# fp32 loads for heads 0 to 3, masks built by query third, and FFN matmuls split into four 32-column tiles, in a block-sparse attention and FFN kernel

## The chip, the cores and the metric

The kernel runs on one core of one Trainium2 chip. The metric is the time that the device measures for one execution, in microseconds (us); lower is better. The profiler's span of an execution is some 2 us shorter than that time. Runs come with a state: "slow" when the time is more than 1.5% above the fastest run of the same kernel, otherwise "fast".

Engines in the profile: PE is TensorE (matmuls), PEld its weight loads, ACT ScalarE, DVE VectorE, POOL GpSimd, SP SyncE, which here issues DMAs only. L214 is a line of the kernel's source; the line numbers differ between kernels.

## The reference

```python
def attention(q, k, v, sampled_blocks):     # q, k, v: (4 batches, 8 heads, 768, 64), fp32
    scores = q @ k^T / 8
    # mask of 32x32 blocks: the diagonal and its neighbours, first and last block row and column,
    # and three blocks per row that sampled_blocks names
    attn = softmax(where(mask, scores, -1e9))
    return attn @ v

def ffn(x, w1, w2, w3, w_out):              # x: (3072 tokens, 512); d_ff = 1024
    return ((x @ w1) * (x @ w2)) @ w3 @ w_out

out = ffn(attention(...) with heads side by side, ...)      # (3072, 512), fp32
```

(Shortened to the formulas.) The mask depends on the sampled blocks, so the kernel has to build it on the chip.

## The kernel before

Everything runs in one program whose order on PE, ScalarE and VectorE is the order of the source. It is a loop of 72 attention steps, 18 for each batch. A step takes four heads, a third of the queries (256) and a third of the keys (256). Loads and the order on GpSimd are left to the scheduler. GpSimd issues the loads of q, k, v and the weights, with a cast from fp32 to bf16.

```python
# step s (cut): scores of this group, then values of the group before, then two pieces of fill
for s, g in enumerate(groups):
    scores(b, t, Q, kp, 0)          # 4 score matmuls for heads 0,1: 64 rows x 128 columns
    scores(b, t, Q, kp, 1)          # 4 for heads 2,3; each call: exp on ScalarE, mask * e on VectorE
    if prev is not None:
        values(*prev)               # 24 matmuls in 128x32 tiles, four heads side by side
        finish(prev)                # after every third group: normalize()
    if b + 1 < B and r in (2, 5, 8, 11):
        load_pair_t(b + 1, (r - 2) // 3)        # next batch: q, k turned by DMA transposes
    if b == 0 and s in (7, 8):
        transposes(0, s - 5)                    # 12 PE transposes and one copy
    pop(0 if s < 3 else 2)                      # fill: weight folding, then the FFN
    prev = g

# normalize(): ln = Ln(d); rec = Exp(-ln)  on ScalarE;  x = o * rec  on VectorE
# The next step's values() overwrite o and d, so they wait for x.

# one FFN piece of the fill (cut): four full 128x128 matmuls of 512 columns
for c in range(4):
    nc.tensor.matmul(p, lhsT=w1_sb[:, c, f * 128:(f + 1) * 128], rhs=x[:, c, :],
                     start=c == 0, stop=c == 3)

# before the first step (cut): block adjacency matrix A (24 x 24) by 21 small VectorE operations,
# expansion G = A * hot (PE, copied by VectorE), then nine masks, each two matmuls and
#     nc.scalar.copy(mask[:, t, kp, :], mp)
```

A "pa" piece of fill is followed by a "pb" piece, and a step takes the two; the "po" pieces are the second product, also two to a step. w3 and w_out are folded into one matrix (wf) first, by fill in the early steps. What is left of the FFN after the last step runs alone: the tail.

The softmax here doesn't subtract the row's maximum and nothing guards it: scores larger than these inputs give would overflow.

## Time and profile before

| | before |
|---|---|
| time, median of 4 runs | 289.2 us (288.57 to 289.72) |
| span of the profiled run | 286.8 us |
| first score matmul | 19.88 us |
| step 5 starts | 33.17 us |
| step 21 starts | 83.91 us |
| step 71, the last, starts | 244.38 us |
| tail, step 71 to the end | 42.4 us |

The checkpoints are read from the trace: a step starts with its first score matmul. FFN pieces begin at step 19 in this kernel, and at step 21 in the changed one.

The windows table of the kernel before (window; its length; busy time of PE, PEld, DVE, ACT and POOL with their instructions; mean clock; DMA share; GB/s) shows the steady part and the tail:

```profile
85.00:240.00 155.00, 153.09 (x1936) 76.76 (x1927) 109.82 (x161) 122.99 (x162) 21.71 (x28) 1.00 0.52 67
240.00:290.00 50.00, 42.57 (x262) 18.79 (x259) 20.05 (x30) 13.74 (x23) 0.00 (x0) 0.96 0.11 43
```

PE is busy 153.09 of 155 us and no other engine is above 123. Busy is not streaming, though. The timeline of PE in one plain step (start, busy time, engine, line, operation, output and inputs, tile rows*columns, operand shapes, count):

```profile
151.28 0.61 PE L214 MATMUL s<-qkt 64*128 64x256 bf16 x8
151.82 0.40 PE L244 MATMUL o<-e,vn 128*32 128x256 bf16 x8
...
152.37 0.28 PE L241 MATMUL d<-e,ones 128*32 128x256 bf16 x4
152.59 1.90 PE L324 MATMUL po<-wf_sb,h 128*128 128x512 bf16 x8
154.42 0.28 PE L214 MATMUL s<-qkt 64*128 64x256 bf16 x2
```

Read the starts. The step is 154.42 - 151.28 = 3.14 us. From single records: four score pairs at 109 ns, six value groups of four tiles at 109 ns (so four 32-column tiles do run side by side), and eight FFN matmuls at 216 ns give 2.82 us. The rest, 0.3 us, is three stops of 0.090 to 0.106 us, one at each change of the tile shape. The Trainium skill, "TensorEngine Tiling (Array Packing)", Key Properties, says that changing the tiling mode drains the engine; it gives no price, and the trace gives one.

Every third step follows a normalise and takes 3.33 us. In the timeline of the kernel before, one such step:

```profile
144.33 0.42 ACT L259 ACTIVATE rec<-ln 128x256 f32<-128x256 f32 x1
144.78 0.69 DVE L260 TENSOR_TENSOR x<-o,rec 128x512 bf16<-128x512 f32 x1
...
144.80 0.61 PE L214 MATMUL s<-qkt 64*128 64x256 bf16 x8
...
145.53 0.40 PE L244 MATMUL o<-e,vn 128*32 128x256 bf16 x8
```

The values start 0.73 us after the scores, where a plain step has 0.54 (151.82 - 151.28): x ends at 145.47, and the values cannot start before. That chain (exp 1.02 us, ln 0.39, rec 0.42, x 0.69) hangs on the *step before*, not on this one's matmuls.

The start, in the timeline of the kernel before (in brackets: idle time before it, and what ended it):

```profile
10.58 0.60 PE L167 MATMUL gp<-hot,Ab 24*24 24x512 bf16 x1 [10.58 <-DVE Ab L161]
...
15.59 4.22 ACT L177 CAST mask<-mp 128x512 bf16<-128x512 f32 x8 [13.57 <-PE mp L175]
...
19.88 1.03 PE L214 MATMUL s<-qkt 64*128 64x256 bf16 x8
```

The adjacency matrix is ready at 10.58 us, the masks hold ScalarE until 19.81, and only then do the scores start.

### The profile page before, as it was taken

Reading aid. Unit: us, or ns where it says so; the run is one execution under the profiler, and the core shown is the slowest. Engines: PE = TensorE matmul, PEld = TensorE weight load, DVE = VectorE, ACT = ScalarE, POOL = GpSimd, SP = SyncE. Lnnn points to the kernel's source line nnn. Section 1 sums busy time; section 2 is a strip of 40 time slices with the busy share of each in tenths; the row PEclk is TensorE's granted clock in tenths of the full one; section 3 lists DMA queues with packets and bytes.
Section 4 is the critical chain, followed back from the end, with each engine's and each line's share of the span. In section 5 each row is a group of like instructions: output and inputs, shape, how many; then the busy total and the mean of one; then the engine's idle time right before and its main releaser. Section 6 shows DMA issues by size and latency. Waiting matters only on the chain.

```text
span 286.8 us, 7359 instructions
## 1 busy us (share of the span) xinstructions
PE 260.8 (91%) x3124; PEld 132.3 (46%) x3124; DVE 183.8 (64%) x296; ACT 188.8 (66%) x250; POOL 71.5 (25%) x105
## 2 busy tenths in 40 slices
PE   0478888898999999999999999999999999999994
PEld 0334555454544454445444554445444544444441
DVE  2616786786767776777677767766776677633332
ACT  1088764776788886888877888768887688611310
POOL 8614489374644820066000000000000000000000
PEclk9986999999999999999999999999999999999998
DMA  7999999999999992399912000121000220003003
GB/s 92 151 190 206 208 174 167 178 119 140 135 167 112 144 109 91 79 118 150 160 73 75 2 2 0 39 75 38 3 2 0 77 75 2 0 37 112 0 29 117
DMA packets 70356, 26.16 MB, mean 91 GB/s; under 512 B 58036, under 2 KB 65204, under 8 KB 70324
## 3 DMA queue, kind: packets, MB, share of 16 engines
q0 software_dynamic: 47632, 14.69, 50.9%
q1 hardware_dynamic: 22692, 11.02, 18.5%
q8 instruction: 24, 0.39, 0.6%
q14 instruction: 8, 0.07, 0.1%
HBM read 29.36 MB, written 6.29 MB: 124 GB/s over the span
## 4 chain that ended last, share of the span: by engine, by line
PE 62%; DMA 12%; ACT 12%; DVE 5%; POOL 5%; issue 3%; POOLq 0%; ACTq 0%
PE pa L303 13%; PE o L244 12%; PE pb L314 12%; DMA w_sb<-in_moe_w_dram 11%; PE po L324 10%; ACT e L219 7%; PE s L214 7%; DVE x L260 4%; PE d L241 4%; PE wp L285 3%; ACT rec L259 3%; ACT ln L257 2%; DMA nt<-in_q_dram 2%; POOL w_sb L99 1%; POOL vn L85 1%
## 5 line engine op out<-in xcount | busy, mean ns | idle before, releaser
L219 ACT ACTIVATE e<-s 128x1024 bf16<-128x1024 f32 x144 | 139.1, 1021 | 47.7 <-PE s L214 47.6
L220 DVE TENSOR_TENSOR e<-e,mask 128x1024 bf16<-128x1024 bf16 x144 | 99.0, 691 | 53.8 <-ACT e L219 53.8
L244 PE MATMUL o<-e,vn 128*32 128x256 bf16 x1152 | 54.7, 277 | 5.4 <-DVE x L260 1.7
L214 PE MATMUL s<-qkt 64*128 64x256 bf16 x576 | 46.8, 277 | 3.5 <-ACT e L219 3.5
L303 PE MATMUL pa<-x,w_sb 128*128 128x512 bf16 x192 | 49.7, 381 | 0.0
L314 PE MATMUL pb<-x,w_sb 128*128 128x512 bf16 x192 | 49.2, 379 | 0.0
L316 DVE TENSOR_TENSOR h<-pb,a 128x512 bf16<-128x512 f32 x48 | 33.1, 690 | 20.9 <-PE pb L314 20.9
L324 PE MATMUL po<-wf_sb,h 128*128 128x512 bf16 x192 | 44.5, 380 | 0.0
L306 ACT CAST a<-pa 128x512 bf16<-128x512 f32 x48 | 28.0, 582 | 22.6 <-PE pa L303 22.2
L241 PE MATMUL d<-e,ones 128*32 128x256 bf16 x576 | 42.5, 275 | 0.0
L214 PEld LDWEIGHTS <-qkt 64*128 64x128 bf16 x576 | 22.8, 95 | 34.7 <-issue 32.0
L244 PEld LDWEIGHTS <-vn 128*32 128x32 bf16 x1152 | 27.5, 96 | 22.0 <-issue 19.2
L314 PEld LDWEIGHTS <-w_sb 128*128 128x128 bf16 x192 | 18.7, 98 | 24.1 <-issue 2.6
L201 POOL DMA_DIRECT2D nt<-in_q_dram x24 | 19.7, 824 | 40.2 <-DMA qkt<-nt 35.9
L324 PEld LDWEIGHTS <-h 128*128 128x128 bf16 x192 | 17.5, 98 | 22.3 <-issue 3.4
L303 PEld LDWEIGHTS <-w_sb 128*128 128x128 bf16 x192 | 15.7, 98 | 21.7 <-issue 8.0
L329 DVE COPY ob<-po 128x512 f32<-128x512 f32 x24 | 16.5, 688 | 10.1 <-PE po L324 10.1
L201 POOL DMA_DIRECT2D nt<-in_k_dram x24 | 19.6, 821 | 4.3 <-DMA qkt<-nt 2.3
L260 DVE TENSOR_TENSOR x<-o,rec 128x512 bf16<-128x512 f32 x24 | 16.6, 692 | 1.6 <-ACT rec L259 0.9
L241 PEld LDWEIGHTS <-ones 128*32 128x32 bf16 x576 | 17.3, 98 | 0.3
L285 PE MATMUL wp<-wo_sb,w3t_sb 128*128 128x512 bf16 x64 | 15.2, 380 | 0.0
L177 ACT CAST mask<-mp 128x512 bf16<-128x512 f32 x9 | 4.8, 587 | 13.7 <-PE mp L175 13.7
(56 smaller groups left out, 106.9 us busy)
## 6 DMA issues: line engine op xcount, KB each, us to landing
out_dram<-ob SPq DMA_DIRECT2D x24, 256.0 KB, 2.0
vn<-in_v_dram POOLq DMA_DIRECT2D x16, 192.0 KB, 5.8
nt<-in_q_dram POOLq DMA_DIRECT2D x24, 96.0 KB, 5.6
nt<-in_k_dram POOLq DMA_DIRECT2D x24, 96.0 KB, 5.6
w_sb<-in_moe_w_dram POOLq DMA_DIRECT2D x8, 256.0 KB, 11.2
w_sb<-in_moe_w_dram POOLq DMA_DIRECT2D x16, 128.0 KB, 5.8
wo_sb<-in_moe_w_out_dram POOLq DMA_DIRECT2D x1, 1024.0 KB, 12.0
qn<-in_q_dram POOLq DMA_DIRECT2D x4, 192.0 KB, 7.2
```

The lines of the kernel that those rows point to most:

```text
L201: nc.gpsimd.dma_start(out=n[:, :, h, :], in_=src[b][:, :, 2 * pr + h, :])
L214: nc.tensor.matmul(s[:, h, k2 * QT:(k2 + 1) * QT], lhsT=qk[64 * h:64 * h + 64, 1, kc * 128:(kc + 1) * 128], rhs=qk[64 * h:64 * h + 64, 0, ...
L219: nc.scalar.activation(e, s, AF.Exp, scale=1.0 / 8.0)
L220: nc.vector.tensor_tensor(e, e, mask[:, t, kp:kp + 1, :].to_broadcast((128, 2, 512)), op=ALU.mult)
L241: nc.tensor.matmul(d[rows, :], lhsT=ones, rhs=rhs, start=first, stop=last, skip_group_check=True)
L244: nc.tensor.matmul(o[rows, part * QT:(part + 1) * QT], lhsT=vn[b, 2 * Q + i][:, h, kc, 32 * part:32 * part + 32], rhs=rhs, start=first and ...
L260: nc.vector.tensor_tensor(X[i][:, 2 * Q:2 * Q + 2, half * QT:(half + 1) * QT], o.rearrange("p (s n) -> p s n", s=2), rec.to_broadcast((128 ...
L303: nc.tensor.matmul(p, lhsT=w1_sb[:, c, f * 128:(f + 1) * 128], rhs=x[:, c, :], start=c == 0, stop=c == 3)
L306: nc.scalar.copy(a, p)
L314: nc.tensor.matmul(p, lhsT=w2_sb[:, c, f * 128:(f + 1) * 128], rhs=x[:, c, :], start=c == 0, stop=c == 3)
L316: nc.vector.tensor_tensor(hT[:, f, :], p, box["a"], op=ALU.mult)
L324: nc.tensor.matmul(box["o"], lhsT=hT[:, f, n * 128:(n + 1) * 128], rhs=wf_sb[:, f, :], start=f == 0, stop=f == NF - 1)
```

## The change

It has three aims: start the attention earlier, by loads without cast from SyncE's queue, a cheaper adjacency matrix and only one third of the masks before the first step; take one shape change out of each step, by running the FFN in the same 128x32 tile shape as the value product; and split the last copy and store. In return some work moves into the steps. The diff, cut to its core:

```diff
+    for pr in range(2):                       # fp32 q and k of heads 0 to 3, from SyncE
+        ...
+            nc.sync.dma_start(out=t, in_=src[0][:, 2 * pr:2 * pr + 2])
-    load_pair(0, 0, "qk")                     # GpSimd's queue, with cast
-    load_pair(0, 1, "qk")
 ...
+    A = const.tile([NB, NB], F32, tag="A")    # adjacency by GpSimd, random blocks by VectorE
+    nc.gpsimd.memset(A, 0.0)
+    ...
+    for base, pat, mul in (...five...):
+        nc.gpsimd.affine_select(out=A, in_=A, compare_op=ALU.not_equal, fill=1.0, base=base, ...)
+    for r in range(3):
+        nc.vector.scalar_tensor_tensor(Ab if r == 2 else A, in0=JJ, scalar=rand_f[:, r:r + 1], ...)
-    DD = ...                                  # the 21 VectorE operations: removed
 ...
+    def mm4(out_, lhsT, rhs, start, stop):
+        for g in range(4):
+            nc.tensor.matmul(out_[32 * g:32 * g + 32, :], lhsT=lhsT[:, 32 * g:32 * g + 32],
+                             rhs=rhs, start=start, stop=stop, skip_group_check=True)
 ...
-                    nc.tensor.matmul(p, lhsT=w1_sb[:, c, f * 128:(f + 1) * 128], rhs=x[:, c, :],
-                                     start=c == 0, stop=c == 3)
+                    mm4(p, w1_sb[:, c, f * 128:(f + 1) * 128], x[:, c, :], c == 0, c == 3)
 ...                                           # the same for w2 and for po
+                    if i == B * NT // 2 - 1 and n == 3:      # the very last block: two halves
+                        nc.scalar.copy(ob[:, :256], box["o"][:, :256])
+                        nc.scalar.dma_start(out=outv[b, c][:, :256], in_=ob[:, :256])
+                        nc.vector.tensor_copy(ob[:, 256:], box["o"][:, 256:])
+                        nc.sync.dma_start(out=outv[b, c][:, 256:], in_=ob[:, 256:])
 ...
-    transposes(0, 0); transposes(0, 1)
-    for t in range(NT): build_mask(t)         # all nine masks
+    ...casts on ScalarE and VectorE, transposes(0, 0), expand(0), masks of the first third...
 ...
-        if b + 1 < B and r in (2, 5, 8, 11):
+        if s == 9:
+            load_pair(1, 0); load_pair(1, 1); load_w12(w1); load_w12(w2)
+            load_pair_t(1, 2); load_pair_t(1, 3)
+        elif 0 < b < B - 1 and r in (2, 5, 8, 11):
             load_pair_t(b + 1, (r - 2) // 3)
+        if s in (1, 3):                       # the other two thirds of the masks
+            expand((s + 1) // 2)
+            for k_ in range(3):
+                build_mask((s + 1) // 2, k_, nc.vector.tensor_copy)
+        if s in (15, 16):
+            transposes(1, s - 15, [nc.vector.tensor_copy])
-        pop(0 if s < 3 else 2)
+        pop(0 if s < 5 else 2)
```

More of the change, by code (lines that the diff above doesn't have):

```diff
@@ L76 @@
     qn, kn, vn = {}, {}, {}
-    rand_sb = const.tile([NB, 6], I32, tag="rand_sb")
-    nc.sync.dma_start(out=rand_sb, in_=sampled_blocks.bitcast(I32))
+    rand_sb = const.tile([NB, 3, 2], I32, tag="rand_sb")
+    nc.sync.dma_start(out=rand_sb, in_=sampled_blocks.bitcast(I32).rearrange("e (r w) -> e r w", w=2))
     def load_pair(b, pr, which="qkv"):
@@ L86, in load_pair @@
                 dst[b, pr] = t
+    raw = {}
+    for pr in range(2):
+        both = hpool.tile([128, 2, 1024], F32, tag="h", name="raw")
+        for x, (src, tag) in enumerate(((qv, "q"), (kv, "k"))):
+            t = both[:, x, :2 * C * D].rearrange("p (h c d) -> p h c d", h=2, c=C)
+            nc.sync.dma_start(out=t, in_=src[0][:, 2 * pr:2 * pr + 2])
+            raw[tag, pr] = t
     w1_sb = wts.tile([128, 4, d_ff], BF16, tag="w1")
@@ L99, in load_w12 @@
                 nc.gpsimd.dma_start(out=t[32 * g:32 * g + 32, 2 * Q:2 * Q + 2, :], in_=src[g][:, Q])
-    load_pair(0, 0, "qk")
-    idf = const.tile([128, 128], F32, tag="idf")
+    idf = const.tile([128, 128], BF16, tag="idf")
     nc.gpsimd.iota(idf, pattern=[[-1, 128]], base=0, channel_multiplier=1,
-                   allow_small_or_imprecise_dtypes=True)
-    load_pair(0, 1, "qk")
-    hotf = const.tile([NB, C, 128], F32, tag="hotf")
-    nc.gpsimd.iota(hotf, pattern=[[1, C], [C, 128]], base=0, channel_multiplier=-BLK,
                    allow_small_or_imprecise_dtypes=True)
@@ L112 @@
                    allow_small_or_imprecise_dtypes=True)
-    II = const.tile([NB, NB], F32, tag="II")
-    nc.gpsimd.iota(II, pattern=[[0, NB]], base=0, channel_multiplier=1,
+    A = const.tile([NB, NB], F32, tag="A")
+    nc.gpsimd.memset(A, 0.0)
+    nc.gpsimd.memset(A[:, 0:1], 1.0)
+    nc.gpsimd.memset(A[:, NB - 1:NB], 1.0)
+    for base, pat, mul in ((0, -1, 1), (1, -1, 1), (-1, -1, 1), (0, 0, 1), (1 - NB, 0, 1)):
+        nc.gpsimd.affine_select(out=A, in_=A, compare_op=ALU.not_equal, fill=1.0, base=base,
+                                pattern=[[pat, NB]], channel_multiplier=mul)
+    hotf = const.tile([NB, C, 128], BF16, tag="hotf")
+    nc.gpsimd.iota(hotf, pattern=[[1, C], [C, 128]], base=0, channel_multiplier=-BLK,
                    allow_small_or_imprecise_dtypes=True)
@@ L117 @@
     load_pair(0, 1, "v")
-    wo_v = moe_w_out.rearrange("(c r) f -> r c f", r=128)
-    nc.gpsimd.dma_start(out=wo_sb, in_=wo_v)
+    nc.gpsimd.dma_start(out=wo_sb, in_=moe_w_out.rearrange("(c r) f -> r c f", r=128))
     def load_w3(lo, hi):
@@ L123, in load_w3 @@
             nc.gpsimd.dma_start(out=w3_sb[:, i, :], in_=moe_w3[128 * i:128 * i + 128, :])
-    load_w3(0, 2)
+    load_w3(0, 3)
     load_pair(0, 2)
-    load_w3(2, 4)
+    load_w3(3, 4)
     load_pair(0, 3)
     load_w3(4, NF)
-    load_w12(moe_w1, w1_sb)
-    load_w12(moe_w2, w2_sb)
     ident = const.tile([128, 128], BF16, tag="ident")
@@ L136 @@
     nc.vector.memset(ones, 1.0)
+    rand_f = const.tile([NB, 3], F32, tag="rand_f")
+    nc.vector.tensor_copy(rand_f, rand_sb[:, :, 0])
+    Ab = const.tile([NB, NB], BF16, tag="Ab")
+    for r in range(3):
+        nc.vector.scalar_tensor_tensor(Ab if r == 2 else A, in0=JJ, scalar=rand_f[:, r:r + 1],
+                                       in1=A, op0=ALU.is_equal, op1=ALU.max)
     hot = const.tile([NB, C, 128], BF16, tag="hot")
@@ L141 @@
     nc.vector.tensor_tensor(hot, hot, hot_hi, op=ALU.mult)
-    DD = const.tile([NB, NB], F32, tag="DD")
-    nc.vector.tensor_sub(DD, II, JJ)
-    A = const.tile([NB, NB], F32, tag="A")
-    nc.vector.tensor_tensor(DD, DD, DD, op=ALU.mult)
-    nc.vector.tensor_scalar(A, in0=DD, scalar1=1.0, scalar2=None, op0=ALU.is_le)
-    for src in (II, JJ):
-        for val, op in ((0.0, ALU.is_le), (float(NB - 1), ALU.is_ge)):
-            t1 = small.tile([NB, NB], F32, tag="m24", name="m24")
-            nc.vector.tensor_scalar(t1, in0=src, scalar1=val, scalar2=None, op0=op)
-            nc.vector.tensor_max(A, A, t1)
@@ L153 @@
-    rand_f = const.tile([NB, 3], F32, tag="rand_f")
-    for r in range(3):
-        nc.vector.tensor_copy(rand_f[:, r:r + 1], rand_sb[:, 2 * r:2 * r + 1])
-        t1 = small.tile([NB, NB], F32, tag="m24", name="m24")
-        nc.vector.tensor_tensor(t1, JJ, rand_f[:, r:r + 1].to_broadcast((NB, NB)),
-                                op=ALU.is_equal)
-        nc.vector.tensor_max(A, A, t1)
-    Ab = const.tile([NB, NB], BF16, tag="Ab")
-    nc.vector.tensor_copy(Ab, A)
     hot2 = hot.rearrange("e c p -> e (c p)")
@@ L164, with expand @@
     G = const.tile([NB, S], BF16, tag="G")
-    gp = ps_s.tile([128, 2, 512], F32, tag="s", name="gp")
-    for i, (lo, n) in enumerate(((0, 512), (512, 256))):
-        nc.tensor.matmul(gp[:NB, i, :n], lhsT=Ab, rhs=hot2[:, lo:lo + n], start=True, stop=True)
-        nc.vector.tensor_copy(G[:, lo:lo + n], gp[:NB, i, :n])
     mask = const.tile([128, NT, 3, 512], BF16, tag="mask")
-    def build_mask(t):
-        for kp in range(3):
-            mp = ps_f.tile([128, 512], F32, tag="f", name="mp")
-            for k2 in range(2):
-                nc.tensor.matmul(mp[:, k2 * QT:(k2 + 1) * QT], lhsT=hot[:, 2 * kp + k2, :],
-                                 rhs=G[:, t * QT:(t + 1) * QT], start=True, stop=True)
-            nc.scalar.copy(mask[:, t, kp, :], mp)
+    def expand(t):
+        gp = ps_f.tile([128, 512], F32, tag="f", name="gp")
+        nc.tensor.matmul(gp[:NB, :QT], lhsT=Ab, rhs=hot2[:, t * QT:(t + 1) * QT],
+                         start=True, stop=True)
+        nc.vector.tensor_copy(G[:, t * QT:(t + 1) * QT], gp[:NB, :QT])
@@ L180, with build_mask, transposes @@
+    def build_mask(t, kp, copy):
+        mp = ps_f.tile([128, 512], F32, tag="f", name="mp")
+        for k2 in range(2):
+            nc.tensor.matmul(mp[:, k2 * QT:(k2 + 1) * QT], lhsT=hot[:, 2 * kp + k2, :],
+                             rhs=G[:, t * QT:(t + 1) * QT], start=True, stop=True)
+        copy(mask[:, t, kp, :], mp)
     QK = {}
-    def transposes(b, pr):
+    def transposes(b, pr, copies):
         tp = ps_s.tile([128, 2, 1024], BF16, tag="s", name="tp")
@@ L189, in transposes @@
         t = qkt.tile([128, 2, S], BF16, tag="qkt", name="qkt")
-        nc.vector.tensor_copy(t, tp[:, :, :S])
+        if len(copies) == 1:
+            copies[0](t, tp[:, :, :S])
+        else:
+            for x, copy in enumerate(copies):
+                copy(t[:, x, :], tp[:, x, :S])
         QK[b, pr] = t
@@ L313, in go @@
                 for c in range(4):
-                    nc.tensor.matmul(p, lhsT=w2_sb[:, c, f * 128:(f + 1) * 128], rhs=x[:, c, :],
-                                     start=c == 0, stop=c == 3)
+                    mm4(p, w2_sb[:, c, f * 128:(f + 1) * 128], x[:, c, :], c == 0, c == 3)
                 nc.vector.tensor_tensor(hT[:, f, :], p, box["a"], op=ALU.mult)
@@ L323, in go @@
                 for f in range(4 * half, 4 * half + 4):
-                    nc.tensor.matmul(box["o"], lhsT=hT[:, f, n * 128:(n + 1) * 128],
-                                     rhs=wf_sb[:, f, :], start=f == 0, stop=f == NF - 1)
+                    mm4(box["o"], hT[:, f, n * 128:(n + 1) * 128], wf_sb[:, f, :],
+                        f == 0, f == NF - 1)
                 if half == 1:
@@ L328, in go @@
                     ob = opool.tile([128, 512], F32, tag="ob", name="ob")
-                    nc.vector.tensor_copy(ob, box["o"])
-                    nc.sync.dma_start(out=outv[b, c], in_=ob)
+                    if i == B * NT // 2 - 1 and n == 3:
[3 more added lines that the diff above has]
+                        nc.sync.dma_start(out=outv[b, c][:, 256:], in_=ob[:, 256:])
+                    else:
+                        nc.vector.tensor_copy(ob, box["o"])
+                        nc.sync.dma_start(out=outv[b, c], in_=ob)
             return go
@@ L338, in ffn @@
             fill.append(po(n, 1))
-    transposes(0, 0)
-    transposes(0, 1)
-    for t in range(NT):
-        build_mask(t)
+    for pr in range(2):
+        for tag, dst in (("q", qn), ("k", kn)):
+            t = nat.tile([128, 2, C, D], BF16, tag=tag + "n", name=tag + "n")
+            (nc.vector.tensor_copy if pr == 0 and tag == "k" else nc.scalar.copy)(t, raw[tag, pr])
+            dst[0, pr] = t
+        if pr == 0:
+            expand(0)
+            transposes(0, 0, [nc.vector.tensor_copy, nc.scalar.copy])
+            for kp in range(3):
+                build_mask(0, kp, nc.scalar.copy if kp == 0 else nc.vector.tensor_copy)
+    transposes(0, 1, [nc.vector.tensor_copy])
     groups = []
@@ L383 @@
             finish(prev)
-        if b + 1 < B and r in (2, 5, 8, 11):
-            load_pair_t(b + 1, (r - 2) // 3)
-        if b == 0 and s in (7, 8):
-            transposes(0, s - 5)
-        pop(0 if s < 3 else 2)
+        if s == 9:
+            load_pair(1, 0)
+            load_pair(1, 1)
+            load_w12(moe_w1, w1_sb)
+            load_w12(moe_w2, w2_sb)
+            load_pair_t(1, 2)
+            load_pair_t(1, 3)
+        elif 0 < b < B - 1 and r in (2, 5, 8, 11):
+            load_pair_t(b + 1, (r - 2) // 3)
+        if s in (1, 3):
+            expand((s + 1) // 2)
+            for k_ in range(3):
+                build_mask((s + 1) // 2, k_, nc.vector.tensor_copy)
+        if s in (7, 8):
+            transposes(0, s - 5, [nc.vector.tensor_copy])
+        if s in (15, 16):
+            transposes(1, s - 15, [nc.vector.tensor_copy])
+        pop(0 if s < 5 else 2)
         prev = g
```

## The prediction

> **What bounds the kernel now.** TensorE. In the windows table, PE is busy 39.5 of every 40 us from 80 to 240 us, VectorE 28 and ScalarE 31 to 32. The timeline gives the loop: one attention step takes 3.145 us, every third one (a normalise) 3.33 us. A plain step is eight 64-row score matmuls (four pairs, 109 ns a pair), 24 value matmuls in 128x32 tiles (six groups of four, 109 ns a group: four tiles do run side by side) and eight 128x128x512 FFN matmuls (216 ns each): about 2.81 us of streaming. The rest is three stops of 0.09 to 0.11 us where the tile shape changes. The Trainium skill, "TensorEngine Tiling (Array Packing)", Key Properties, says a change of tiling mode drains the array; the trace agrees, about 0.1 us each. In the normalise step the chain of waits leaves PE: exp 1.02, ln 0.4, reciprocal 0.43, multiply 0.70, so the values start 3.88 us after the scores, 0.19 us later than PE could.
>
> **Ends.** First score matmul at 19.9 us, after masks and casts-by-DMA; the tail after the last step is about 42 us of pure FFN.
>
> **FFN split.** Four 32-column tiles of 512 columns should take 216 ns together, as one full matmul does, so no gain in the tail. In mixed steps the value-to-FFN switch (0.106 us) disappears. The FFN runs in steps 21 to 71; in the normalise third, the exp-ln-multiply chain still sets the time and swallows it. Gain: 34 x 0.106 = 3.6 us. About 3,450 more PE instructions; the value groups already issue as densely, so no cost.
>
> **Start.** Raw loads land early, but the ScalarE and VectorE order makes the adjacency matrix come last: its five selects on GpSimd stand between DMA issues of 0.5 to 0.9 us each, so I estimate it ready near 8 us, first scores near 16 us, exp about 4 us earlier than before.
>
> **Given back.** (a) Masks of thirds 1 and 2 now stand in steps 1 and 3: each time PE waits for VectorE (G copy 0.4, mask copies 0.69 each) and ScalarE starves: about 3 us each, 6 us together, against 4.2 us of mask copies removed from the start. (b) Fill begins at step 5 instead of 3: four FFN pieces (two pa/pb pairs, 1.87 us each in the tail now) move to the tail, +3.75 us. (c) PE transposes for batch 1, pairs 0 and 1: the same work costs about 2.75 us at steps 7 and 8 now; the same again at steps 15 and 16. (d) Split last copy: -0.3 us.
>
> **Sum.** Step 21 starts about 1 us later than the 83.9 us of before (early first step, minus a, minus two steps without fill, minus c); then -3.6, +3.75, -0.3: within a microsecond or two of unchanged. Predicted 289.0 us; range 284 to 294. Chances: faster by over 2% 0.13, within 2% 0.79, slower by over 2% 0.08.
>
> **What would show it.** Plain steps of about 3.04 us and normalise steps still 3.33; no gap between value and FFN matmuls; FFN groups of four 216 ns apart; the first score near 16 us; PE gaps of 2 to 3 us in steps 1 and 3; step 21 near 85 us; a tail longer by about 3.5 us.
>
> **What would make it wrong.** FFN tiles sharing one moving operand may not stream side by side (much slower: each 1% of the 216 ns costs 1.2 us); the start may be far quicker than 16 us if the selects don't queue behind DMA issues (2 to 3 us faster); VectorE may absorb the mask copies; the normalise chain may shorten too (1.8 us more); the late weight loads or the batch-1 loads may arrive after step 21.

## More of the kernel before

From the page of the kernel before: busy time of each engine with its share of the span and its instructions; the granted PE clock in tenths over 40 slices; and the DMA queue that fetches instructions (packets, MB, share).

```profile
PE 260.8 (91%) x3124; PEld 132.3 (46%) x3124; DVE 183.8 (64%) x296; ACT 188.8 (66%) x250; POOL 71.5 (25%) x105
...
PEclk9986999999999999999999999999999999999998
...
q8 instruction: 24, 0.39, 0.6%
```

PE is the bound, and the average hides how much so.

## The result, and the profile after

| | before | after |
|---|---|---|
| time, median of 4 runs | 289.2 us (288.57 to 289.72) | 289.97 us (289.88 to 290.14) |
| span of the profiled run | 286.8 | 288.1 (+1.3) |
| first score matmul | 19.88 | 14.51 (-5.37) |
| step 5 starts | 33.17 | 33.26 (+0.09) |
| step 21 starts | 83.91 | 84.90 (+0.99) |
| step 71 starts | 244.38 | 241.89 (-2.49) |
| tail | 42.4 | 46.2 (+3.8) |

The ratio of the times is 1.0028 (95% interval 1.0008 to 1.0049): the same, at a threshold of 2%. Ratios in this text are the mean time of one kernel's fast runs over the mean of the other's in the same rounds, so they are not quite the ratio of the medians that are quoted. The checkpoints in brackets are differences from the kernel before at that point, and they show that the change did not do nothing: it won 5.4 us, lost it within five steps, won 3.5 us in the steady part, and lost that in the tail.

The page of the kernel after, the same three lines:

```profile
PE 261.4 (91%) x4893; PEld 149.4 (52%) x4901; DVE 188.0 (65%) x291; ACT 186.2 (65%) x247; POOL 65.9 (23%) x104
...
PEclk9999999999999999999999999999999999999999
...
q8 instruction: 38, 0.62, 0.9%
```

PE has 1,769 more records and is busy 0.6 us longer: four tiles take the time of one full matmul. The instruction fetches went from 24 to 38. (The PEclk row is not to be believed at its left end, see below.) The windows table of the kernel after:

```profile
85.00:240.00 155.00, 151.12 (x3168) 87.73 (x3170) 112.61 (x165) 123.83 (x167) 14.21 (x18) 1.00 0.44 60
240.00:290.00 50.00, 44.23 (x803) 23.89 (x792) 19.11 (x28) 12.76 (x22) 0.00 (x0) 0.98 0.12 44
```

**The steady part.** The PE timeline of the kernel after, in the same stretch as before:

```profile
151.34 0.40 PE L245 MATMUL o<-e,vn 128*32 128x256 bf16 x8
...
151.89 0.28 PE L242 MATMUL d<-e,ones 128*32 128x256 bf16 x4
152.00 1.90 PE L297 MATMUL po<-wf_sb,h 128*32 128x512 bf16 x32
153.83 0.61 PE L215 MATMUL s<-qkt 64*128 64x256 bf16 x8
```

From the last "d" group to the FFN it is now 0.11 us (152.00 - 151.89), the streaming time of that group; before it was 0.22 (152.59 - 152.37). The stop is gone, and a plain step takes 3.04 us. The 32 tiles take 1.83 us (153.83 - 152.00), as the eight full matmuls did (154.42 - 152.59). In single records the four tiles of a group start within 10 ns and the groups 216 ns apart.

The step after a normalise takes 3.34 us, as before (3.33). In the timeline of the kernel after:

```profile
144.06 0.42 ACT L260 ACTIVATE rec<-ln 128x256 f32<-128x256 f32 x1
...
144.42 0.61 PE L215 MATMUL s<-qkt 64*128 64x256 bf16 x8
144.51 0.69 DVE L261 TENSOR_TENSOR x<-o,rec 128x512 bf16<-128x512 f32 x1
...
145.26 0.40 PE L245 MATMUL o<-e,vn 128*32 128x256 bf16 x8 [0.23 <-DVE x L261]
```

The values now start 0.84 us after the scores (145.26 - 144.42), where it was 0.73. The 0.11 us that the FFN gave up, the wait for x took.

**The start.** The timeline of the kernel after:

```profile
3.78 0.22 POOL L123 TENSOR_SCALAR_AFFINE_SELECT A<-A 24x24 f32<-24x24 f32 x1
3.93 0.89 POOL L131 DMA_DIRECT2D wo_sb<-in_moe_w_out_dram  x1
...
6.28 0.22 POOL L123 TENSOR_SCALAR_AFFINE_SELECT A<-A 24x24 f32<-24x24 f32 x1
6.53 0.50 DVE L151 SCALAR_TENSOR_TENSOR A<-JJ,rand_f,A 24x24 f32<-24x24 f32 x2 [4.19 <-POOL A L123]
...
8.50 0.36 PE L165 MATMUL gp<-hot,Ab 24*24 24x256 bf16 x1 [8.50 <-DVE hot L157]
```

The scheduler put load issues of 0.56 to 0.89 us between the five selects of 0.22 us on GpSimd, so VectorE waited 4.19 us for the matrix. Still, the first scores come 5.37 us earlier than before.

**Where the early start went.** The timeline of the kernel after, in step 1:

```profile
19.90 0.41 DVE L167 CAST G<-gp 24x256 bf16<-24x256 f32 x1
20.36 1.00 PE L172 MATMUL mp<-G,hot 24*128 24x256 bf16 x4 [0.50 <-DVE G L167]
20.98 2.05 DVE L174 CAST mask<-mp 128x512 bf16<-128x512 f32 x3 [0.67 <-PE mp L172]
...
22.88 1.02 ACT L220 ACTIVATE e<-s 128x1024 bf16<-128x1024 f32 x1 [3.74 <-PE s L215]
```

PE does its work in program order, so the next scores stand behind the expansion and six mask matmuls, which wait for VectorE's copies in turn. ScalarE is idle 3.74 us before the next exp, and 3.61 us in step 3. Second, the PE clock. The PE timeline of the kernel after, the scores of steps 5 and 6:

```profile
33.26 1.03 PE L215 MATMUL s<-qkt 64*128 64x256 bf16 x8
...
36.00 0.61 PE L215 MATMUL s<-qkt 64*128 64x256 bf16 x8
```

Eight score matmuls take 1.03 us in the steps up to step 5, and 0.61 from 36 us on. So PE ran at half rate until then. The first clock record of this trace is at 35.2 us (half to full); before it there is none, so the PEclk row shows full clock, wrongly. In the kernel before, the row dips to 6: its records say half rate from 19.0 to 25.9 us. The Trainium skill, "TensorE: Matmul & The Clock Gate", Part 1 (The HAM clock gate), tells of a half-rate default that about 3.4 us of sustained work lifts and an idle window restores, and warns that the trace's clock events can be unreliable. The trace agrees with a half rate at the start (1.03 against 0.61 us) and with the warning. The recorded stretches between two early clock changes last 3.4, 6.8, 10.2 or 13.7 us, multiples of 3.4.

### The profile page after: what moved, and what is told of

It reads as the page before. It is cut to its first block, busy times and chain, and to the rows that moved or that the text cites. A ratio compares the mean times of both kernels' runs of the same rounds, so it can differ in the third digit from the quotient of the medians.

```text
span 288.1 us, 10913 instructions
## 1 busy us (share of the span) xinstructions
PE 261.4 (91%) x4893; PEld 149.4 (52%) x4901; DVE 188.0 (65%) x291; ACT 186.2 (65%) x247; POOL 65.9 (23%) x104
## 3 DMA queue, kind: packets, MB, share of 16 engines
HBM read 29.36 MB, written 6.29 MB: 124 GB/s over the span
## 4 chain that ended last, share of the span: by engine, by line
PE 76%; DVE 8%; DMA 6%; ACT 4%; issue 4%; POOL 2%; ACTq 0%; POOLq 0%
PE pb L297 15%; PE po L297 14%; PE pa L297 14%; PE o L245 13%; PE s L215 8%; PE d L242 5%; DVE x L261 5%; PE wp L286 4%; DMA vn<-in_v_dram 3%; ACT e L220 3%; DMA w_sb<-in_moe_w_dram 2%; DMA nt<-in_q_dram 1%; PE tp L184 1%; DVE e L221 1%; PE mp L172 1%
## 5 line engine op out<-in xcount | busy, mean ns | idle before, releaser
L245 PE MATMUL o<-e,vn 128*32 128x256 bf16 x1152 | 56.7, 284 | 5.4 <-DVE x L261 3.9
L297 PEld LDWEIGHTS <-w_sb 128*32 128x32 bf16 x1536 | 44.2, 97 | 33.4 <-issue 3.8
L297 PE MATMUL pa<-x,w_sb 128*32 128x512 bf16 x768 | 50.2, 379 | 0.0
L297 PE MATMUL pb<-x,w_sb 128*32 128x512 bf16 x768 | 50.1, 379 | 0.0
L297 PE MATMUL po<-wf_sb,h 128*32 128x512 bf16 x768 | 44.6, 379 | 0.0
L297 PEld LDWEIGHTS <-h 128*32 128x32 bf16 x768 | 21.9, 97 | 16.2
L202 POOL DMA_DIRECT2D nt<-in_q_dram x20 | 16.4, 827 | 41.2 <-DMA qkt<-nt 41.2
L202 POOL DMA_DIRECT2D nt<-in_k_dram x20 | 16.3, 822 | 8.2 <-DMA qkt<-nt 6.2
L85 POOL DMA_DIRECT2D vn<-in_v_dram x16 | 11.5, 722 | 3.2 <-DMA vn<-in_v_dram 2.3
L260 ACT ACTIVATE rec<-ln 128x256 f32<-128x256 f32 x24 | 10.0, 417 | 0.8
```

The lines of the kernel that those rows point to most:

```text
L202: nc.gpsimd.dma_start(out=n[:, :, h, :], in_=src[b][:, :, 2 * pr + h, :])
L245: nc.tensor.matmul(o[rows, part * QT:(part + 1) * QT], lhsT=vn[b, 2 * Q + i][:, h, kc, 32 * part:32 * part + 32], rhs=rhs, start=first and ...
L297: nc.tensor.matmul(out_[32 * g:32 * g + 32, :], lhsT=lhsT[:, 32 * g:32 * g + 32], rhs=rhs, start=start, stop=stop, skip_group_check=True)
```

## The experiments

Twelve kernels ran, and all gave correct results. "After plus" means the changed kernel with one more edit. "Span" and the checkpoints come from the profiled run of each. The two main theories: (T1) the parts of the change give and take as the prediction's sum says; the rival (T2) is that the split itself has a hidden cost, or that some part does nothing.

### b_split: the kernel before, with the FFN split alone

The edit is mm4 from the diff above, and its three uses; nothing else.

> The kernel before with nothing changed but the FFN matmuls split into four 32-column tiles. My theory: one mode switch of 0.106 us disappears from every plain step with FFN work (steps 19 to 71, 35 or 36 of them plain), the normalise steps stay at 3.33 us, the tail stays: 3.7 us faster, ratio to before about 0.987. Rival 1, that 3,450 more PE instructions cost issue time: plain steps no shorter than 3.145 us or the tail longer, ratio 1.00 or more. Rival 2, that every step gains: 53 x 0.106 = 5.6 us, ratio 0.980.

Measured: median 286.12 us, ratio to before 0.9887 (0.987 to 0.9903). The profiled run was slow (336.25 us, at a granted clock of 0.863), so its trace is not read. The split alone gives 3.2 us, half a microsecond less than expected. It is a gain without any of the rest.

### a_nosplit: after, with full FFN matmuls

```diff
     def mm4(out_, lhsT, rhs, start, stop):
-        for g in range(4):
-            nc.tensor.matmul(out_[32 * g:32 * g + 32, :], lhsT=lhsT[:, 32 * g:32 * g + 32], ...)
+        nc.tensor.matmul(out_, lhsT=lhsT, rhs=rhs, start=start, stop=stop)
```

> The changed kernel with the FFN matmuls whole again, all else as changed. My theory: plain steps back to 3.145 us from step 21 on, 34 x 0.106 = 3.6 us slower than the changed kernel, near 293.5 us, ratio to before 1.015. If the split were worth nothing, 290 us; if its worth shows only together with the other parts, this run and the split alone will not agree in size.

Measured: median 292.85 us, ratio to before 1.0122 (1.0107 to 1.0137). Plain steps are 3.145 us again and post-normalise steps 3.33; steps 21 to 71 take 160.5 us instead of 157.0, while step 21 starts at 84.88 as in after. With b_split this fences the split in from both sides: about 3 us. The trace says why it is not 3.5: in the tail the split costs 0.28 us (the last matmul starts 41.96 us after step 71 in after, 41.68 in a_nosplit), so 3.49 - 0.28 = 3.2 us are left. And everything else in the change together costs some 3.6 us (292.85 against 289.27 for before in the same rounds).

### a_order: after, with the FFN pieces ahead of the values in the step that follows a normalise

```diff
+        early = s > 20 and s % 3 == 1
+        if early:
+            pop(2)
         if prev is not None:
             values(*prev)
...
-        pop(0 if s < 5 else 2)
+        pop(0 if s < 5 or early else 2)
```

> The changed kernel, but in the step that follows a normalise the two FFN pieces are issued before the value matmuls, from step 22 on. Same matmuls, same tiles. My theory: the values of that step wait 0.39 us for the exp-ln-reciprocal-multiply chain, and the FFN pieces fill that wait, so all steps become about 3.04 us: 17 x 0.30 = 5 us faster than changed, near 285 us, ratio about 0.985. Rival: the chain also holds up something else (exp, or the 32-column copy order on ScalarE), so that the wait moves on to the next step and the gain is under 1.5 us.

Measured: median 286.28 us, ratio 0.9898 (0.9883 to 0.9912). Steps after a normalise take 3.04 to 3.12 us instead of 3.34; steps 21 to 71 take 153.3 us instead of 157.0. So the wait for x did swallow the split's gain there: once PE has other work while x is computed, the gain appears. The expectation was 5 us; 3.7 came. The trace shows where most of the missing 1.3 us went: PE stops for 0.76 us in step 39 with no recorded wait. Such stops come back below.

### a_mask: after, with the late masks one at a time

```diff
+        if s in (0, 3):
+            expand(s // 3 + 1)
         scores(b, t, Q, kp, 0)
...
-        if s in (1, 3):
-            expand((s + 1) // 2)
-            for k_ in range(3):
-                build_mask((s + 1) // 2, k_, nc.vector.tensor_copy)
+        if s < 6:
+            build_mask(s // 3 + 1, s % 3, nc.vector.tensor_copy)
```

> The changed kernel, but the mask tiles of thirds 1 and 2 are built one per step in steps 0 to 5, and the 24-row expansions stand before the scores of steps 0 and 3. Same instructions in total. My theory: PE no longer waits behind a burst of VectorE copies; steps 1 and 3 fall from 6.0 and 6.3 us to 2 to 3 us, step 5 starts 7 to 8 us earlier and the kernel ends 7 us or more earlier, near 282.5 us, ratio 0.977. Rival A: the early steps are slow because the matmuls run at half rate there, not because of the masks: then steps 1 and 3 still fall, but steps 2 and 4 stay at 2.37 us. Rival B: VectorE is full in these steps, so the copies cost the same wherever they stand: gain under 2 us.

Measured: median 288.42 us, ratio 0.9959 (0.9938 to 0.9981). A miss in size. Step 1 went from 6.00 to 3.40 us and step 3 from 6.29 to 1.80; step 5 starts 5.4 us earlier (27.85). So the bunching of three masks was the cost, as T1 has it. But half of it did not last: steps 5 and 6 took 4.07 and 4.74 us (PE waits 1.53 us for a mask copy, and the clock record has half rate from 32.4 to 35.8 us), so step 21 is only 2.6 us earlier. And in step 39 the PE timeline of a_mask has this:

```profile
140.00 0.82 PE L297 MATMUL pa<-x,w_sb 128*32 128x512 bf16 x11
142.84 0.61 PE L297 MATMUL pa<-x,w_sb 128*32 128x512 bf16 x5 [2.02 <-issue]
```

The engine stops after 11 of 16 matmuls of one piece for 2.02 us, and "issue" means that it waited for nothing that the profile records: no data, no semaphore. (By the starts, the step of 5.45 us is 2.4 longer than its neighbours; the 2.02 counts from the modelled end of the matmul before.) See the section on the stops.

### a_sel: after, with GpSimd in program order, so that the selects come before the loads

```diff
-        engines={mybir.EngineType.PE, mybir.EngineType.Activation, mybir.EngineType.DVE}
+        engines={mybir.EngineType.PE, mybir.EngineType.Activation, mybir.EngineType.DVE,
+                 mybir.EngineType.Pool}
```

> The changed kernel with GpSimd held to program order: the five selects of the adjacency matrix come before the first load that GpSimd issues, instead of one between each two loads. My theory: the matrix is ready near 3.5 us instead of 6.5, VectorE's hot matrices near 5.5 instead of 8.4, and the first scores stand near 11.7 us instead of 14.5; nothing later takes the gain back, so 2.8 us faster than changed, near 287 us. Rival: the loads of q and k (landed near 4 to 6 us) or the ScalarE casts set the start: gain under 1 us.

Measured: median 287.54 us, ratio 0.9944 (0.9913 to 0.9976), span 285.4, 2.7 less than after. The timeline of a_sel:

```profile
2.78 0.50 DVE L152 SCALAR_TENSOR_TENSOR A<-JJ,rand_f,A 24x24 f32<-24x24 f32 x2 [0.44 <-POOL A L124]
...
11.42 0.61 PE L216 MATMUL s<-qkt 64*128 64x256 bf16 x4
```

GpSimd's part of the matrix is ready 3.75 us earlier than in after (2.78 against 6.53), the first scores come 3.1 us earlier, and the end 2.7 us. Nearly all of an earlier start reaches the end.

### a_swdge: after, with q and k of heads 0 to 3 loaded by GpSimd with cast again

```diff
-            nc.sync.dma_start(out=t, in_=src[0][:, 2 * pr:2 * pr + 2])      # and the four casts
+    load_pair(0, 0, "qk")
+    load_pair(0, 1, "qk")
```

> The changed kernel with heads 0 to 3 of q and k loaded by GpSimd with the cast in the load, as before, and no casts on ScalarE and VectorE. My theory: the worth of the SP loads is GpSimd's time: four more issues of 0.7 to 0.8 us stand before the selects, so the matrix is ready near 9.5 us; but ScalarE's casts of 0.84 us each for the second pair (1.7 us on the way to the first scores) go away: first scores near 15.5 us, 1 us later than changed, 1 us slower in all. Rival, that the earlier landing of raw loads is the worth: first scores 3 us later or more.

Measured: median 292.69 us, ratio 1.0122 (1.0092 to 1.0153). A miss in size: +2.8 us on the span instead of +1. The timeline of a_swdge:

```profile
9.83 0.50 DVE L146 SCALAR_TENSOR_TENSOR A<-JJ,rand_f,A 24x24 f32<-24x24 f32 x2 [4.29 <-POOL A L118]
...
17.52 0.61 PE L210 MATMUL s<-qkt 64*128 64x256 bf16 x4
```

The data was not what the start waited for: PE's transposes of q begin at 12.35 us, behind the matrix's expansion at 12.05, and the trace shows no wait for a load before them. All four loads had landed by 8.5 us, and in after the second pair lands later than here (10.1 and 12.3 us against 7.5 and 8.5). What moves is GpSimd: four more issues stand before its selects, its part of the matrix comes 3.3 us later (9.83 against 6.53), the first scores 3.0. That is the size that the rival named, but its reason, data that land later, is not what the trace shows. The worth of the SyncE loads is not faster data but GpSimd's time. The Trainium skill, "DMA: Bandwidth & Descriptors", section "Issuing engines are not separate DMA queues", says that issuing from other engines only saves the time on the sequencer, "usually small relative to the DMA itself". The first half agrees. The saving was not small here: four issues of 0.72 to 0.84 us, one after the other, ahead of something that the whole start waits for.

### a_fill3: after, with the fill from step 3 as before

```diff
-        pop(0 if s < 5 else 2)
+        pop(0 if s < 3 else 2)
```

> The changed kernel with the filling work begun at step 3 as before, not at step 5. My theory: two pa/pb pairs leave the tail (from 46.2 us after the last step's scores to 42.4, 3.8 us shorter), steps 3 and 4 grow by 1.5 to 2.5 us together: 1.5 to 2 us faster than changed. Rival: the longer steps take all of it: same time.

Measured: median 290.77 us, ratio 1.006 (1.0032 to 1.0088). A miss, with the wrong sign. The tail is 42.4 us again (-3.8) as expected, and step 21 starts 2.94 us later (87.84), so the fill's shift is worth about 0.9 us net. PE stops in steps 38 and 40 (1.47 and 0.76 us) turn that into a loss.

### a_dmat: after, with DMA transposes for batch 1, pairs 0 and 1

```diff
         if s == 9:
-            load_pair(1, 0); load_pair(1, 1)
+            load_pair_t(1, 0); load_pair_t(1, 1)
...
-        if s in (15, 16):
-            transposes(1, s - 15, [nc.vector.tensor_copy])
```

> The changed kernel with pairs 0 and 1 of batch 1 transposed by DMA instead of on PE at steps 15 and 16. My theory: steps 15 and 16 take 6.48 us together instead of 8.47, 2.0 us faster than changed, near 288 us, if the transposed tiles arrive before step 18 (75 us), which they should since the first batch-1 tiles arrived by 65 us before. Rival: the DMA queues are the limit of the first 80 us; then step 18 waits and nothing or a loss is seen.

Measured: median 288.88 us (one of four runs slow), ratio 0.999 (0.996 to 1.0021). Steps 15 and 16 take 6.48 us together instead of 8.47: the PE transposes cost 2.0 us, not the 2.75 of the prediction. It pays 0.66 back in step 10 and 0.45 in step 40, both in stops without a recorded wait (see below); the span is 1.4 lower.

### a_warm: after, plus 70 small matmuls whose result nobody reads, ahead of the first real one

```diff
+    for _ in range(70):
+        nc.tensor.matmul(warm_t[:, :128], lhsT=ident, rhs=ident, start=True, stop=True)
```

> The changed kernel with 70 extra matmuls of 128 columns, whose result nobody reads, on PE in the first 8 us, where PE only waits. Question: are the early steps slow because of the clock? In the changed kernel the clock record begins at 35.2 us, and pairs of 256-column score matmuls stand 0.21 us apart until then, 0.11 after. Theory: if the burst brings the full clock and the following work keeps it, steps 2 and 4 fall from 2.37 to 1.87 us and the other early steps by a few tenths each: 2 to 3 us faster than changed. My expectation is that the clock falls back during the mask bursts, as it did at 19 us in the kernel before, so steps 3 to 5 stay slow and under 1.5 us are gained. If the time does not move and the spacing stays 0.21, the burst did not raise the clock and the test says nothing.

Measured: median 290.73 us (289.14 to 292.41), ratio 1.0055 (1.0007 to 1.0102). The clock went to full from 5.7 to 12.5 us, back to half until 26.1, full to 29.6, half to 36.4. Steps 2 and 4 still took 2.37 us; step 5 started 0.6 us earlier. So the half clock is not cured by a burst ahead, perhaps because PE is too idle in the prologue to keep it; and as steps 2 and 4 stayed at half rate, no run shows what the full clock would be worth there. Of the extra 2.5 us of span, stops in steps 38 and 40 make 2.3.

### c_best, c_whole and c_pet: what the runs pointed to, put together

c_best is after plus the edits of a_sel, a_dmat and a_fill3, the early FFN of a_order (from step 19), and masks one per step:

```diff
+            expand(1)                          # in the prologue, after the first third's masks
     transposes(0, 1, [nc.vector.tensor_copy])
+    expand(2)
...
+        if s < 6:
+            build_mask(s // 3 + 1, s % 3, nc.vector.tensor_copy)   # ahead of the scores
         scores(b, t, Q, kp, 0)
```

> Everything that the earlier runs recommend: the changed kernel with the selects first, one mask tile per step placed before the scores (expansions in the prologue), filling work from step 3, DMA transposes for all of batch 1, and the FFN pieces before the values after each normalise. From the single runs: selects -2.7, masks -2.6 or better, order -5 without the instruction wait, transposes -1.5, fill -1: 12 us faster than changed, near 278 us, ratio 0.963. If the waits for instructions at steps 38 to 40 come back in full, 2 to 3 us slower than that; if the early gains overlap (all compete for the same cold first 35 us), 281.

Measured: median 281.98 us, ratio 0.9678 (0.9645 to 0.9711) on two fast runs (279.64 and 280.07; 283.88 and 285.95 count as slow). The fast runs lie between the 278 and the 281 of the expectation, but where runs spread like this, over 6 us, the 1.5% rule cuts through a range, and the interval is too narrow. The first scores come at 13.31 us, but step 21 takes 4.18: PE waits for a pair of batch 1, which now comes through a DMA transpose, as the timeline of c_best has it:

```profile
82.75 0.39 PE L216 MATMUL s<-qkt 64*128 64x256 bf16 x4 [0.97 <-DMA qkt<-nt]
```

c_whole is c_best with full FFN matmuls (the edit of a_nosplit).

> The same as the combined kernel, but with whole 128-column FFN matmuls. Here no normalise wait can swallow the split, so every step with FFN work should lose 0.10 us by the whole matmuls: 52 steps, 5.2 us slower than the combined kernel, minus whatever that one loses waiting for instructions at steps 38 to 40; the PE fetches 24 instruction blocks instead of 38, so I expect no such wait in this one. If the wait appears here too, the extra instructions are not its cause.

Measured: median 284.86 us, ratio 0.9882 (0.9822 to 0.9942) on three fast runs. Steps 22 to 71 take 154.1 us against 150.1 in c_best, so the split is worth 4.0 us there, as all post-normalise steps gain too once the order hides x. (c_best gives 0.78 us away in step 43, where VectorE's copy waits for an output store, as in c_pet below.) The fast runs differ by 2.1%, with the caution just given; the profiled spans differ by 2.1 us. These steps take 3.145 us, and no stop appears in steps 36 to 45.

c_pet is c_best with the PE transposes of after instead of a_dmat's part.

> The combined kernel, but with the PE transposes of the change kept for pairs 0 and 1 of batch 1. The combined kernel's trace waited 1.1 us at step 21 for a DMA-transposed pair, and its runs spread over 6 us. My theory: with eight DMA transposes less in the crowded first 90 us, step 21 does not wait and the spread narrows to about 2 us; PE pays 2.0 us at steps 15 and 16, so the best run is 1 us slower than the combined kernel's best (279.6), near 280.5 to 281, and the median about the same as or better than its 282. If the spread stays at 6 us, the DMA transposes of batch 1 are not its cause.

Measured, in six runs: median 279.5 us (277.94 to 281.03, and one slow run of 283.9), ratio to before 0.9664 (0.9631 to 0.9697). It is the best kernel: 3.4% less time than before, and by the medians 3.6% less than after. Step 21 no longer waits (3.04 us). The spread did not fall to the 2 us expected: with the slow run it is still 6 us, so by the expectation's own test the DMA transposes of batch 1 are not its cause; the cause stays open. The span is 277.5, 10.6 less than after: 4.5 by step 21 (80.39), 2.3 from there to step 71, 3.8 in the tail. It has a wait of its own in step 43, which takes 5.28 us. The lines of SyncE's queue in c_pet, and then lines of its timeline:

```profile
124.37 23.53 SPq L204 DMA_TRANSPOSE qkt<-nt  x8
147.99 3.40 SPq L341 DMA_DIRECT2D out_dram<-ob  x4
```

```profile
150.34 0.69 DVE L340 COPY ob<-po 128x512 f32<-128x512 f32 x1 [2.11 <-DMA out_dram<-ob]
...
151.09 1.05 PE L298 MATMUL pb<-x,w_sb 128*32 128x512 bf16 x16 [2.06 <-DVE ob L340]
```

Eight transposes stand in SyncE's queue until 147.99 us, and the output stores stand behind them. The transposes take SyncE 1.2 to 1.9 us each, 11 us together; for the rest of the 23.5 us SyncE waits, mostly for the loads that they turn. VectorE's copy waits for a store to free its buffer, and PE for VectorE. Issuing the stores from another engine is the next thing to try; no run here did.

### The stops without a recorded wait

| kernels | FFN split | PE stops in steps 36 to 45, us |
|---|---|---|
| before, a_nosplit, c_whole | no | 0 |
| after, a_sel, a_swdge | yes | 0 |
| a_order, a_dmat | yes | 0.76; 0.45 (and 0.66 in step 10) |
| a_mask | yes | 2.4 |
| a_fill3, a_warm | yes | 1.47 + 0.76; 0.65 + 1.66 |
| c_best | yes | 0 (but 1.18 in step 10) |

They stand in the middle of a group of like matmuls. Those of steps 36 to 45 are in split kernels alone, though not in all of these. (b_split has no usable trace, and the long step 43 of c_best and c_pet has a recorded wait.) The one thing that the split adds besides matmuls is instructions: 38 blocks fetched instead of 24. The Trainium skill, "Runtime: NRT & Kernel Launch", section "Instruction fetch mechanics", says that an engine's instructions come in 16 KiB blocks of 256 by DMA, and that crossing a block is "mostly hidden". The block size agrees (0.62 MB in 38 fetches). Normally a block is fetched every 6.2 us or so in the steady part.

The traces say where the stops are. Count PE's records, matmuls and weight loads, that start before the matmul that ends a stop. In a_order, a_dmat, a_mask, a_fill3 and a_warm the count is 4,282, and for the second stop of a_fill3 and of a_warm it is 4,538, just 256 more. (Not every instruction is recorded, so the distance tells, not the count.) It is so in a_warm too, although its 70 extra matmuls and their weight loads come first. So the stops keep to a number of instructions, not to a place in the program. Each of them ends 1.3 to 2.0 us after the end of a fetch, the 16th or 17th of its trace; in the same traces the blocks from the 18th on had landed 3.7 to 7.0 us before PE came to their first record. Together this makes a block that came late the likely cause. The PE timeline of c_best, step 10:

```profile
49.00 0.40 PE L246 MATMUL o<-e,vn 128*32 128x256 bf16 x6 [0.90 <-issue]
```

This stop and the one of a_dmat in step 10 stand at 958 and 960 records, close to 4,282 - 13 x 256 = 954, and end 1.4 and 1.5 us after the third fetch. No split matmul has run by step 10, so such a stop doesn't need the split.

Why the blocks came late is less clear. In a_mask there is a pause in the fetches from 128.1 to 139.3 us, just ahead of the stop at 140.8; in a_warm one fetch of 2.26 us starts at 145.1, and PE stops from 147.2 to 148.7. The DMA engines are busy then: the DMA row of a_mask's page stands at 9 from 122 to 144 us. But after has a pause of 8.2 us there and no stop. This is an inference from times side by side: no run delayed a fetch alone, so the cause is not shown by experiment. For the rivals, this means: T1's sum accounts for the changed kernel, whose trace has no such stop; of T2's hidden cost it has the 0.28 us in the tail.

## Why the prediction was right

It said 289.0 us, 284 to 294, most likely within 2%; it was 289.97, ratio 1.0028. Point by point:

- **The split pays about 3.6 us: right.** The trace has -3.48 us between steps 21 and 71, which is 33 plain steps times 0.106; b_split alone gave 3.2, as the split costs 0.28 us in the tail. Plain steps take 3.04 as predicted, and the tail's matmuls the same 216 ns.
- **The normalise step swallows its share: right**, 3.34 us, with the mechanism that was named. a_order shows it: with other work ahead of the values, these steps fell to 3.04 to 3.12.
- **The tail grows by 3.75 us: right**, +3.8, and a_fill3, with the fill back at step 3, takes away just that. The split last copy gives -0.2 instead of -0.3: the last matmul starts 4.27 us before the end instead of 4.51. That gain and the split's loss in the tail cancel.
- **The start: mechanism right, size off.** The selects do stand between load issues, and a_sel gains 2.7 us by taking them out, within the 2 to 3 that the prediction named. But GpSimd's part of the matrix was ready at 6.5 us and the whole at 7.3, not 8, and the first scores came at 14.51, not 16: a gain of 5.4 instead of 3.9. How this gain divides between the loads, the cheaper matrix and the fewer masks no run shows; putting the loads back (a_swdge) costs 3.0 of it.
- **The masks in steps 1 and 3: mechanism right, term too small.** 6 us was predicted; ScalarE's two waits are 3.74 + 3.61 = 7.35. a_mask shows that they shrink when the masks are spread (step 5 starts 5.4 us earlier), though half of that was lost again in steps 5 and 6.
- **Missed: the half clock.** In after, PE stays at half rate until about 35 us. Steps 2 and 4 take 2.37 us instead of the 1.87 of a short step at full rate: 1.0 us together that no term had. That is an estimate: no run changed the clock alone there.
- **The steps without fill, and the transposes: both too large.** Leaving the fill out of steps 3 and 4 was to save 3.75 us; the two steps took 2.84 and 3.85 before and would take an estimated 1.87 each without fill, so it saves 2.95. The transposes cost 2.0, not 2.75.
- **"No cost" for the extra instructions: nearly right for this kernel** (no stop in its trace, 0.28 us in its tail), but not in general, if the stops belong to them.

So "about 1 us later at step 21" was exact (+0.99) partly by luck: its errors cancel. The kept run matters too. The runs of before are of two kinds: the profiled one (286.8 us, mean clock 0.985) is of the faster kind; those of the other, recorded at 0.997 to 1.0, span 287.4 to 288.0 us. Against these, after is about 0.6 us longer, not 1.3. The prediction's sum, as far as its terms are given, was -3.9 for the start, +6 - 3.75 = +2.25 for steps 0 to 5, +2.75 for steps 5 to 21: +1.1. The trace has -5.37, +5.46 and +0.90. The start was 1.5 better, the first steps 3.2 worse (masks 1.35, clock 1.0, fill 0.8), and the stretch after them 1.85 better (transposes 0.75; the rest is in steps 8, 19 and 20, 1.3 us shorter with other pieces of fill in them, less 0.2 in steps 5 and 6). The total of such a sum deserves more trust than its terms only when the terms were checked, as they were here afterwards.

The result is "the same" because two real gains met two real costs of like size, and neither cost was needed: c_pet keeps the gains, undoes the costs by order alone, and is 3.4% faster than before.

## What to carry to other kernels

Where matmuls of different tile shapes alternate in a loop, look for pauses at the change of shape, and give neighbours the same shape if the streaming time stays the same; then ask in which steps another chain ends last, because the gain is lost there until independent work is moved ahead of that wait. When work is moved out of a prologue, spread it one piece a step, ahead of what it must not delay, and keep the filler work starting where it did, or the tail pays it back. Judge a bundle by checkpoints along the span, not by its total: a total near zero can be 9 us of gains and 10 us of losses.

## What the Trainium skill lacked or had wrong

- "TensorEngine Tiling (Array Packing)", Key Properties, says that a mode change drains the engine but gives no price. Here each change between 64x128, 128x32 and 128x128 tiles cost 0.090 to 0.106 us, and removing one of three gave 1.1% of the kernel's time (b_split).
- "TensorE: Matmul & The Clock Gate", section "Back-to-back issue gap", gives about 131 ns for each 512-column matmul sustained in a stream with weight loads, and 216 ns for an isolated one, although Part 1 of the same page has 215.7 ns measured back to back. In these streams nearly every 512-column matmul, or group of four 32-column ones, takes 216 ns, in the middle of eight and through a tail of 42 us: what Part 1 has, and not the 131 ns.
- The same page, Part 1, warns that clock events can be unreliable, but not that the state before the first event can be missing. Here there is no record before the first change: the changed kernel ran at half rate until 35.2 us, and the profile's row and its mean clock (0.999) show full clock for that time. The duration of eight like matmuls (1.03 against 0.61 us) is the safer sign.
- "Runtime: NRT & Kernel Launch", "Instruction fetch mechanics", calls the crossing of a block mostly hidden. Six kernels with 10,800 to 11,100 recorded instructions had PE stops of 0.4 to 2.4 us without a recorded wait. In five of them these stand at counts of PE's records that are equal or 256 apart. Late blocks are the likely cause; why they came late is not shown.
- No page was found that warns of plain stores that stand behind DMA transposes on one issuing engine. In c_pet eight transposes, 11 us of issue and 12.5 us mostly of waiting for their inputs, stood in SyncE's queue for 23.5 us, and the output stores behind them cost PE 2.06 us.
